# Attention and two feed-forward networks on one core: block 0 goes through both networks before the pair

## The chip, the core and the metric

The kernel runs on one core of a Trainium2 chip. The metric is the device time of one execution in microseconds. A core has TensorE (matmuls, PE below), VectorE (DVE), ScalarE (ACT), GpSimd (POOL) and SyncE (SP, whose one queue issues all transfers here). Every engine works through its own instructions in a fixed order and waits at semaphores for the others.

## The reference

Three stages in a row, all with float32 results:

```python
# 1 attention, 2 x 8 heads, 768 positions, 64 wide: a window of |i-j| < 16, and 24 block keys
k_sum = k.reshape(B, H, 24, 32, D).max(axis=3);  v_sum = v.reshape(B, H, 24, 32, D).mean(axis=3)
scores = concat(where(|i-j| < 16, q @ k.T / 8, -1e9), q @ k_sum.T / 8 + log(32))
x = softmax(scores) @ concat(v, v_sum)                       # 1536 tokens x 512
# 2 gated network, 512 -> 1536 -> 512
xn = x / sqrt(mean(x * x) + 1e-6) * rms_g
g = xn @ w_gate;  x = (g * sigmoid(g) * (xn @ w_val)) @ w_out
# 3 second network, 512 -> 2048 -> 512
h = x @ w_in;  out = where(h > 0, h, exp(min(h, 0)) - 1) @ w_out2
```

The five weight matrices arrive as 64-bit floats.

## The kernel before, in words

**Blocks.** The 1536 tokens are three blocks of 512. Block 0 goes through the first network alone (12 chunks of 128 hidden columns: g and v projections, gate, down product). Blocks 1 and 2 go through it as a *pair*: the up products are made by seven products of sums of parts instead of eight plain ones (Strassen's scheme in Winograd's form), where the parts are the two blocks and the two halves of the model dimension. For that each chunk needs sums of weight halves (`half_sum`, s1 to s4, four per chunk) and VectorE combines the seven product banks into four results (`add_combine`, seven additions and one copy). The second network is made in the same way: block 0 alone by seven products over its own halves with 256 columns each (`product`, L1084), the pair by seven with 512 columns (`pair_product`, L1237). There the sums of weights are whole tiles (`w_sum`, four per group of four chunks).

**Splitting.** Each factor of a matmul is split into a rounded high part and a remainder (`split_a` and `act_a` on ACT, L303; `split_b` and `act_b`, L314), and each product is three matmuls: high by high, high by low, low by high.

**Weights.** `fetch` loads 512 KB of 64-bit words into one of three staging buffers (`st`), four steps turn them into float32 (`convert_a` on ACT L432; `convert_b` L440 and `convert_d` L453 on VectorE), `keep` stores the tile in device memory, and `again` loads it back for a later use (`j0i`, `j0p` for block 0's second network, `j1...` for the pair). The first network's weights (g, v, o) are converted while block 0 goes through it; those of the second (i, p) from 40 us after the start of the pair's first network on, one every 5.6 us of the plan.

**Attention** is made in 12 pairs of 64-token tiles. The four pairs of block 0 and a part of the next come first, the others are strewn through block 0's first network, one pair every 14 us of the plan. From the eighth pair on (`HERE = 7`) the queries are loaded by 16 small transfers and transposed on VectorE (L527); before, they are loaded at once, transposed by TensorE (L501) and copied by ACT.

**What sets the order.** No order is written out. Every operation is added to a planner (`class Order`) with an engine (or a choice of engines), a cost, a due time and what it reads and writes; the planner plays the operations through with its own costs, takes on each free engine the ready one that is due first, and issues the instructions in the order that comes out. Due times follow from the starts of the chunks (`chunk1_at`, `joint1_at`, `chunk2_at`, `joint2_at`) and from a table of offsets, `SHIFT`, by operation and stage. The stages of the program are therefore: start and block 0's attention; block 0, first network; pair, first network; block 0, second network; pair, second network.

Of the kernel before, what the change touches and what calls it, by code (L numbers as in the profile page):

```python
# [10 lines left out]
F32 = mybir.dt.float32  # L11
F32R = mybir.dt.float32r
# [9 lines left out]
P = 128  # L22
# [195 lines left out]
def fused_kernel(ctx: ExitStack, tc: tile.TileContext, q, k, v, w_gate, w_val, w_out, rms_g, w_in2, w_out2, out):  # L218
    nc = tc.nc
# [17 lines left out]
    TB = 512  # L237
# [149 lines left out]
    joint1_at = [T0 + LEN_A * C1 + LEN_J * c for c in range(C1)]  # L387
    start2 = T0 + (LEN_A + LEN_J) * C1
    chunk2_at = [start2 + LEN_2 * c for c in range(C2)]
    joint2_at = [start2 + LEN_2 * C2 + LEN_U * u for u in range(U2)]  # L390
    tile_at = {}
    for i in range(B * NQ):
        blk, r = divmod(i, TPB)
        if blk == 0:
            tile_at[i] = A0 + A_GAP * r + (LATER if r >= TPB // 2 else 0) + TOFF[r]
        else:
            tile_at[i] = T0 + TILE8 + GAP_1 * (i - TPB)
# [6 lines left out]
    turn = [(kind, 4 * u + x) for u in range(U2) for kind in "ip" for x in range(4)]  # L404
    weights += [(kind, c, joint1_at[0] + CONV0 + CONV * n) for n, (kind, c) in enumerate(turn)]
# [49 lines left out]
    def add_weights(kind, c, need):  # L455
# [7 lines left out]
        add("SP", 0.75, need - 4, keep, kind, c, r=[raw], w=[f"kept_{kind}{c}"])  # L463
# [629 lines left out]

    def down2(b, u, m, n, first, last):
        ot = T[f"act2_{b}_{u}{m}{n}"]
        for j in range(2):
            wt = T[f"ws{b}_p{4 * u + 2 * m + j}"]
            for q in range(2):
                name = f"acc2_{b}_{2 * n + q}"
                acc = new(f"a{2 * n + q}", name, [P, TB]) if first and j == 0 else T[name]  # L1100
                cs = slice(j * HALF + q * P, j * HALF + (q + 1) * P)
                for x, (a, e) in enumerate(THREE):
                    nc.tensor.matmul(  # L1103
                        acc, ot[:, a, cs], wt[:, e, :],
                        start=first and j == x == 0, stop=last and j == 1 and x == 2)
# [20 lines left out]

    def add_block2():
        b = 0
        names = [f"acc2_{b}_{m}" for m in range(4)]
        src = [f"x1_{b}#n{c}_0" for c in range(KM)]  # L1130
        t0 = chunk2_at[0]

        def halves(name):
            return [f"xt{b}_{name}"] if name[0] == "t" else src[:2] if name[0] == "1" else src[2:]

        add("-", 0.0, t0 - 9, wait, w=[f"begin{b}"])
        for dst, at in (("t1", -3.2), ("t2", -2.6), ("t3", -1.0), ("t4", -0.5)):
            x, y = X_SUMS[dst]
            add(SUM_X, 0, t0 + at, x_sum, b, dst, r=halves(x) + halves(y) + [f"begin{b}"], w=[f"xt{b}_{dst}"], new=[(TMP, f"xt{b}_{dst}")])
        for i in range(7):  # L1140
            xq = f"xq{b}_{i}"
            at = t0 - 4 + 0.9 * i
            add({ACT: 0.52, DVE: 0.34}, 0, at, factor_a, b, i, r=halves(PAIRS[i]) + [f"begin{b}"], w=[xq + "#h"], new=[("x", xq)])
            add(SUM_X, 0, at + 0.5, factor_b, b, i, r=halves(PAIRS[i]) + [xq + "#h"], w=[xq + "#l"])
        for u in range(U2):
            t = chunk2_at[4 * u]
            n = f"{b}_{u}"
            for x in (2, 3, 0, 1):
                add_again(0, "i", 4 * u + x, t - 13 + 0.2 * x)
            add_sums(b, u, t)  # L1150
            tt = [t + STEP * i for i in range(7)]
            p = f"_{n}"
            for i in range(7):
                add_split(f"ws{n}_{i}", weight_of(b, u, i), tt[i], LO_1)
                bank = f"p{i}{p}"
                add(PE, 1.44, tt[i], product, b, u, i, bank, MM + AT,
                    r=[f"ws{n}_{i}#h", f"ws{n}_{i}#l", f"xq{b}_{i}#h", f"xq{b}_{i}#l"], w=[bank],
                    new=[(MM + AT, bank)])
            add_combine(p, tt, MM + AT)
            for k, (m, h, done) in enumerate(((0, 0, 1), (0, 1, 4), (1, 1, 5), (1, 0, 6))):  # L1160
                at = tt[done] + 2.3
                act = f"act2_{n}{m}{h}"
                add_elu(f"c{m}{h}{p}", f"ex{p}{m}{h}", act, at, "t2")
                if k in (0, 2):
                    for j in range(2):
                        x = 4 * u + 2 * m + j
                        add_again(0, "p", x, at + DOWN2[k] - 7)
                        add_split(f"ws{b}_p{x}", f"j0p{x}", at + DOWN2[k] + 0.7 * j, LO_1)
# [224 lines left out]
    for i in range(B * NQ):  # L1393
# [135 lines left out]
```

## Time and profile before

| | us |
|---|---|
| median of 3 runs | 656.55 |
| lowest, highest | 653.52, 662.18 |
| the profiled execution | 656.8 |
| its span in the trace | 655.1 |

| engine | busy us | share of the span |
|---|---|---|
| TensorE | 612.9 | 94% |
| VectorE | 562.1 | 86% |
| ScalarE | 379.2 | 58% |
| GpSimd | 210.2 | 32% |

The granted TensorE clock is 0.992 of full speed over the span. Neighbouring instructions of an engine overlap in the records (the end of one lies behind the start of the next), so the cost of one among others is read from start to start, not from its length. Busy time counts overlapped time once.

### The profile page before, as it was taken

The page shows a single profiled execution, that of the slowest core. Times are in us where ns is not written, and L with a number is a line of the kernel's source. Part 1 is how long each engine was busy: PE and PEld are TensorE (multiplying, and loading weights), DVE is VectorE, ACT ScalarE, POOL GpSimd, SP SyncE. Part 2 cuts the span into 40 slices and gives each one's busy share as a digit, 9 for nine tenths or more (in the row PEclk, how much of TensorE's full clock was granted, in tenths as well). Part 3 has the DMA queues.
Part 4 walks back from the last instruction along what each step waited for, and adds up shares of the span by engine and source line. Part 5 has one row for each costly group of instructions (what it writes and reads, how often), then busy time and mean ns, then how long its engine had stood idle before and what let it go on. Part 6 is the DMA issues. An engine that isn't in the chain of part 4 may idle for free.

```text
span 655.1 us, 10659 instructions
## 1 busy us (share of the span) xinstructions
PE 612.9 (94%) x3668; PEld 497.9 (76%) x3668; DVE 562.1 (86%) x961; ACT 379.2 (58%) x819; POOL 210.2 (32%) x240
## 2 busy tenths in 40 slices
PE   7689999779999999899889899999999999999997
PEld 4478866557778678677778687889887878888885
DVE  4788896569899999999999799989999996498665
ACT  2777866678838445455434545678675753355351
POOL 6763364444534324335225302331430210200000
PEclk9979999999999999999999899999999999999999
DMA  9999778779737238575546253534223211020003
GB/s 210 241 275 215 230 194 215 174 235 252 255 93 218 88 122 280 175 241 194 193 155 215 80 162 125 181 129 138 56 81 130 65 62 52 0 66 0 1 0 130
DMA packets 100454, 97.04 MB, mean 148 GB/s; under 512 B 54192, under 2 KB 69808, under 8 KB 100400
## 3 DMA queue, kind: packets, MB, share of 16 engines
q1 hardware_dynamic: 100400, 96.36, 51.1%
q8 instruction: 29, 0.48, 0.3%
q14 instruction: 25, 0.20, 0.1%
HBM read 75.37 MB, written 20.97 MB: 147 GB/s over the span
## 4 chain that ended last, share of the span: by engine, by line
PE 37%; DVE 29%; issue 3%; DMA 1%; ACT 1%; DVEq 0%
PE p_k L1237 10%; PE dn L1245 8%; PE acc L985 7%; PE acc L1103 5%; PE p L1084 4%; PE p_j L1237 3%; DVE c_j L1092 3%; DVE wj L314 3%; DVE h_j L1092 3%; DVE act_j L314 2%; DVE th_j L956 2%; DVE ws L314 2%; DVE th_j L952 2%; DVE raw_i L453 1%; DVE raw_p L453 1%
## 5 line engine op out<-in xcount | busy, mean ns | idle before, releaser
L1237 PE MATMUL p_j<-xh,wj 128*128 128x512 f32 x336 | 110.6, 395 | 8.3 <-DVE c_j L1092 3.8
L1237 PEld LDWEIGHTS p_j<-xh,wj 128*128 128x128 f32 x336 | 63.0, 188 | 27.3 <-DVE c_j L1092 5.6
L1237 PE MATMUL p_k<-xh,ws 128*128 128x512 f32 x224 | 71.7, 391 | 0.9 <-DVE h_k L1092 0.9
L1237 PE MATMUL p_j<-xl,wj 128*128 128x512 f32 x168 | 65.5, 390 | 0.0
L1237 PEld LDWEIGHTS p_k<-xh,ws 128*128 128x128 f32 x224 | 42.0, 188 | 10.7 <-DVE h_k L1092 1.0
L1277 POOL TENSOR_TENSOR sa<-j1v 128x256 f32<-128x256 f32 x12 | 18.4, 1530 | 92.4 <-DVE wj L314 45.0
L1103 PE MATMUL acc<-ws_p,act 128*128 128x512 f32 x192 | 45.8, 391 | 0.4 <-DVE act L314 0.4
L1245 PE MATMUL dn<-ws_p,act_k 128*128 128x512 f32 x192 | 45.8, 389 | 0.0
L985 PE MATMUL acc<-ws_p,act_k 128*128 128x512 f32 x192 | 45.5, 389 | 0.0
L1084 PEld LDWEIGHTS p<-xq,ws 128*128 128x128 f32 x336 | 42.3, 191 | 2.7 <-issue 1.6
L1084 PE MATMUL p<-xq,ws 128*128 128x256 f32 x336 | 42.9, 283 | 1.4 <-DVE x L1251 1.4
L1237 PE MATMUL p_k<-xl,ws 128*128 128x512 f32 x112 | 43.7, 390 | 0.3 <-DVE xl L1206 0.3
L1245 PEld LDWEIGHTS dn<-ws_p,act_k 128*128 128x128 f32 x192 | 36.0, 188 | 7.6
L985 PEld LDWEIGHTS acc<-ws_p,act_k 128*128 128x128 f32 x192 | 36.0, 188 | 7.5
L1103 PEld LDWEIGHTS acc<-ws_p,act 128*128 128x128 f32 x192 | 35.5, 188 | 7.9 <-DVE act L314 0.9
L948 ACT ACTIVATE th_j<-c_j 128x512 f32<-128x512 f32 x24 | 15.2, 633 | 43.5 <-DVE c_j L1092 43.4
L1245 PE MATMUL dn<-act_j,wjo 128*128 128x512 f32 x144 | 36.5, 406 | 3.0 <-DVE h_j L1092 1.9
L919 PE MATMUL pg<-xs,ws_g 128*128 128x512 f32 (+1 forms) x168 | 37.8, 369 | 0.8 <-POOL ws_g L314 0.8
L1044 POOL TENSOR_TENSOR w_s<-j1i,j1i 128x512 f32<-128x512 f32 x8 | 13.0, 1624 | 78.1 <-DVE ws_p L314 48.6
L985 PE MATMUL acc<-act_j,wjo 128*128 128x512 f32 x144 | 36.2, 391 | 1.2 <-DVE act_j L314 1.2
L985 PE MATMUL acc<-act,ws_o 128*128 128x512 f32 x144 | 36.2, 397 | 0.4 <-DVE act L314 0.2
L1251 DVE TENSOR_TENSOR ob<-ob,dn 128x512 f32<-128x512 f32 x28 | 19.0, 684 | 20.2 <-PE dn L1245 20.2
(292 smaller groups left out, 1568.8 us busy)
## 6 DMA issues: line engine op xcount, KB each, us to landing
st_i<-in_moe_w_in SPq DMA_DIRECT2D x16, 512.0 KB, 4.1
st_p<-in_moe_w_out SPq DMA_DIRECT2D x16, 512.0 KB, 3.8
st_g<-in_moe_w_gate SPq DMA_DIRECT2D x12, 512.0 KB, 4.6
st_v<-in_moe_w_val SPq DMA_DIRECT2D x12, 512.0 KB, 5.9
st_o<-in_moe_w_out SPq DMA_DIRECT2D x12, 512.0 KB, 4.3
kept_i<-raw_i SPq DMA_DIRECT2D x16, 256.0 KB, 2.2
kept_p<-raw_p SPq DMA_DIRECT2D x16, 256.0 KB, 2.3
j0i<-kept_i SPq DMA_DIRECT2D x16, 256.0 KB, 3.1
```

The lines of the kernel that those rows point to most:

```text
L314: (nc.gpsimd if eng == POOL else nc.vector).tensor_sub(out, a, b)
L453: nc.vector.scalar_tensor_tensor(low, rest, 2.0 ** -13, low, op0=ALU.mult, op1=ALU.add)
L919: nc.tensor.matmul(pt[:, i], wt[:, a, kk * P:(kk + 1) * P], xt[:, c, i], start=(kk == 0 and n == 0), stop=(kk == KM - 1 and n == 2))
L948: nc.scalar.activation(out=new(tag, th, [P, TB]), in_=T[pg], func=AF.Tanh, scale=0.5)
L985: nc.tensor.matmul(acc, lhsT, rhs, start=(first and n == 0), stop=(last and n == 2))
L1084: nc.tensor.matmul(pt[:, m * HALF:(m + 1) * HALF], wt[:, a, kk * HALF + m * P:kk * HALF + (m + 1) * P], xt[:, c, kk], start=kk == n == 0, ...
L1092: nc.vector.tensor_add(new(TMP, dst, [P, TB]), T[src], T[other])
L1103: nc.tensor.matmul(acc, ot[:, a, cs], wt[:, e, :], start=first and j == x == 0, stop=last and j == 1 and x == 2)
L1237: nc.tensor.matmul(pt, wt[:, a, cs], xt[e][:, kk], start=kk == n == 0, stop=kk == 1 and n == 2)
L1245: nc.tensor.matmul(pt, lhsT, rhs, start=x == n == 0, stop=x == len(pairs) - 1 and n == 2)
L1251: nc.vector.tensor_add(T[dst][:, m], T[dst][:, m], T[src])
L1277: (e.tensor_add if dst == "s1" else e.tensor_sub)(t[:, i * HALF:(i + 1) * HALF], x, y)
```

## The change

1. **Order of the stages.** Block 0 goes through the first and then the second network, and only then does the pair start: block 0, first; block 0, second; pair, first; pair, second. The second network's weights are fetched and converted in block 0's second network and used there at once, without `again`. Tiles of block 1 lie in block 0's first network, those of block 2 in its second.
2. **Block 0's second up product is plain** (`project2`): per chunk 12 matmuls of 512 columns, no sums, no combining.
3. **Sums of weights on VectorE**: `half_sum` and `w_sum` go from GpSimd to VectorE.
4. **Queries turned by TensorE**: `HERE` from 7 to 12, so all twelve are.
5. **Plan refitted**: `SHIFT`, its stage limits `EDGES`, and some lengths are new; `keep` is issued 3 us behind a weight's need instead of 4 ahead.

```diff
-    SUM_W = {POOL: 1.28}
+    SUM_W = {DVE: 0.6}
-    SUM_H = {POOL: 0.8}
+    SUM_H = {DVE: 0.335}
...
-    joint1_at = [T0 + LEN_A * C1 + LEN_J * c for c in range(C1)]
-    start2 = T0 + (LEN_A + LEN_J) * C1
+    start2 = T0 + LEN_A * C1
     chunk2_at = [start2 + LEN_2 * c for c in range(C2)]
-    joint2_at = [start2 + LEN_2 * C2 + LEN_U * u for u in range(U2)]
+    pair1 = start2 + LEN_2 * C2
+    joint1_at = [pair1 + LEN_J * c for c in range(C1)]
+    joint2_at = [pair1 + LEN_J * C1 + LEN_U * u for u in range(U2)]
...
-    turn = [(kind, 4 * u + x) for u in range(U2) for kind in "ip" for x in range(4)]
-    weights += [(kind, c, joint1_at[0] + CONV0 + CONV * n) for n, (kind, c) in enumerate(turn)]
+    for c in range(C2):
+        weights += [("i", c, chunk2_at[c // 2 * 2] - 2 + 0.8 * (c % 2)), ("p", c, chunk2_at[c] + 4)]
...
-        add("SP", 0.75, need - 4, keep, kind, c, r=[raw], w=[f"kept_{kind}{c}"])
+        add("SP", 0.75, need + KEEP, keep, kind, c, r=[raw], w=[f"kept_{kind}{c}"])
...
+    def project2(name, u, h, m):
+        pt = new(MM, name, [P, TB])
+        for k in range(2):
+            wt = T[f"ws0_i{4 * u + 2 * h + k}"]
+            for kk in range(2):
+                cs = slice(kk * HALF + m * P, kk * HALF + (m + 1) * P)
+                xt = T[f"xa_{2 * k + kk}"]
+                for n, (a, e) in enumerate(THREE):
+                    nc.tensor.matmul(pt, wt[:, a, cs], xt[:, e], start=k == kk == n == 0, stop=k == kk == 1 and n == 2)
...
+        add_x("x1_0", "xa", 0, TB, chunk2_at[0] - 3)
+        x = [f"xa_{kk}#{p}0" for kk in range(KM) for p in "hl"]
+        for c in range(C2):
...
+            add(PE, 2.72, t, project2, ph, u, h, m, r=x + [y + z for y in w for z in ("#h", "#l")], w=[ph], new=[(MM, ph)])
+            add_elu(ph, ex, act, t + 2.8, "t2")
+            add_split(wp, f"raw_p{c}", t + 6, LO_1)
+            add_down(names, act, wp, c == 0, c == C2 - 1, False, t + DOWN2)
...
     add_block1()
+    add_block2()
     add_joint1()
-    add_block2()
     add_joint2()
...
-    ('copy_k', 0): -3, ('copy_keys', 0): -8, ('copy_q', 0): -2, ('diagonal', 0): -8, ('exps', 0): 0.5,
+    ('copy_k', 0): 18.5, ('copy_keys', 0): -11, ('diagonal', 0): 25, ('exps', 0): 28, ('load_q', 0): 3.5,
...
-HERE, KHERE, TURNED, ACT_B = 7, 6, 0.48, 0
+HERE, KHERE, TURNED, ACT_B = 12, 6, 0.48, 0
-LEN_A, LEN_J, LEN_2, LEN_U = 10.5, 15.0, 5.3, 41.0
+LEN_A, LEN_J, LEN_2, LEN_U = 9.3, 15.0, 6.3, 41.0
```

Three places in the instruction order. First VectorE in the middle of the pair's first network (`p_j` are the product banks, `h_j` and `c_j` the partial and finished combinations, `th_j` the gate, `wj` split weights, `sa` and `sb` the half sums, `raw_i` weights under conversion). Before:

```order
L952 SCALAR_TENSOR_TENSOR th_j_3967<-th_j_3967,c_j_3964 128x512
L453 SCALAR_TENSOR_TENSOR raw_i_3933<-st_i_3832,raw_i_3933 128x512
L956 SCALAR_TENSOR_TENSOR th_j_3967<-th_j_3967,c_j_3977 128x512
L314 TENSOR_TENSOR wj_1_3979<-sa_3935,wj_1_3979 128x512
L314 TENSOR_TENSOR wj_2_3990<-sb_3962,wj_2_3990 128x512
L314 TENSOR_TENSOR act_j_4008<-th_j_3967,act_j_4008 128x512
L440 TENSOR_SCALAR raw_i_4026<-st_i_3894 128x512
L314 TENSOR_TENSOR wj_3_4023<-j1v_3761,wj_3_4023 128x256
```

and now:

```order
L1203 TENSOR_TENSOR sb_4148<-j1g_3997,sa_4102 128x256
L1203 TENSOR_TENSOR sa_4151<-j1v_3896 128x256
L1203 TENSOR_TENSOR sb_4148<-j1g_3997,j1v_3988 128x256
L1203 TENSOR_TENSOR sa_4151<-sa_4151,j1g_3907 128x256
L1052 TENSOR_TENSOR h_j_4161<-p_j_4109,h_j_4135 128x512
L1203 TENSOR_TENSOR sb_4165<-j1g_3907,sa_4151 128x256
L314 TENSOR_TENSOR wj_1_4163<-sa_4151,wj_1_4163 128x512
L1203 TENSOR_TENSOR sb_4165<-j1g_3907,j1v_3896 128x256
L1052 TENSOR_TENSOR c_j_4183<-p_j_4168,h_j_4161 128x512
```

The conversions are gone from this stretch, and half sums stand in their place, always ahead of the split that reads them.

Second, TensorE where block 0 leaves the first network (`acc` are the down sums). Before, the pair's products (`p_j`) follow, which read nothing of block 0:

```order
L985 MATMUL acc_0_0_1500<-act_0_8_2527,ws_o_2357 128x512 x3
L985 MATMUL acc_0_1_1504<-act_0_8_2527,ws_o_2357 128x512 x3
L860 MATMUL prs2slice(0, 512, None)_2759<-dg2slice(0, 512, None)h,ones 128x512
L860 MATMUL prs2slice(0, 512, None)_2759<-dg2slice(0, 512, None)l,ones 128x512
L1237 MATMUL p_j_2762<-xh_0_2448,wj_0_2744 128x512
```

and now block 0's own second network (`ph`), whose input `xa` is split from the finished sums:

```order
L974 MATMUL acc_0_0_1230<-act_0_11_2504,ws_o_2314 128x512 x3
L974 MATMUL acc_0_1_1234<-act_0_11_2504,ws_o_2314 128x512 x3
L974 MATMUL acc_0_2_1435<-act_0_11_2504,ws_o_2314 128x512 x3
L974 MATMUL acc_0_3_1439<-act_0_11_2504,ws_o_2314 128x512 x3
L736 MATMUL at_3_0_2566<-ident,e_3_0_2357 120x128 x4
L736 MATMUL at_3_1_2575<-ident,e_3_1_2358 120x128 x4
L502 MATMUL qt_5_2587<-ident,qr_5_2467 128x128 x4
L748 MATMUL pv_3_2597<-ats_3_0_2582,va_179 64x64
...
L1082 MATMUL ph_2623<-xa_2564,ws_i_2377 128x512 x3
```

Between the last sum and the first product that needs it stand three groups of transposes and one tile product.

Third, TensorE where the pair leaves the first network (`dn_11` are the last down sums of block 2, gathered on VectorE). Before, block 0's products (`p_0_0`, `p_0_1`) lie between them:

```order
L1084 MATMUL p_0_0_4869<-xq_5_4533,ws_0_5_4747 128x256 x12
L1084 MATMUL p_0_0_4888<-xq_6_4536,ws_0_6_4777 128x256 x12
L1245 MATMUL dn_11_2_4917<-act_j_4336,wjo_4221 128x512 x3
L1245 MATMUL dn_11_2_4917<-act_j_4511,wjo_4348 128x512 x3
L1245 MATMUL dn_11_2_4917<-act_j_4685,wjo_4635 128x512 x3
L1084 MATMUL p_0_1_4937<-xq_0_4479,ws_1_0_4819 128x256 x12
```

and now the pair's second network (`p_k`), which reads the sums:

```order
L974 MATMUL acc_1_3_3903<-act_j_5265,wjo_5164 128x512 x3
L1171 MATMUL dn_11_1_5305<-act_j_5009,wjo_4915 128x512 x3
L1171 MATMUL dn_11_1_5305<-act_j_5190,wjo_5046 128x512 x3
L1171 MATMUL dn_11_1_5305<-act_j_5262,wjo_5164 128x512 x3
L1171 MATMUL dn_11_2_5324<-act_j_5009,wjo_4915 128x512 x3
L1171 MATMUL dn_11_2_5324<-act_j_5190,wjo_5046 128x512 x3
L1171 MATMUL dn_11_2_5324<-act_j_5262,wjo_5164 128x512 x3
L1163 MATMUL p_k_5340<-xh_0_5303,ws_0_0_5135 128x512
```

18 matmuls of 512 columns stand between block 1's last sum (`acc_1_3`) and the first product of the next network.

## Rows read from the trace of the kernel before

**Rows 1.** Stages: us, busy us (instructions) by engine, clock, DMA share, GB/s

```profile
0.00:49.88 49.88, 38.98 (x506) 28.76 (x507) 34.04 (x80) 30.41 (x102) 33.22 (x86) 0.93 1.08 243
49.88:190.09 140.21, 128.62 (x1083) 102.40 (x1082) 111.53 (x228) 101.78 (x278) 67.29 (x78) 1.00 0.78 210
190.09:387.60 197.51, 186.11 (x805) 148.51 (x804) 192.87 (x311) 98.47 (x179) 65.57 (x48) 0.99 0.54 176
387.60:479.79 92.19, 89.30 (x536) 79.18 (x535) 89.08 (x139) 63.05 (x113) 25.53 (x16) 1.00 0.42 129
479.79:655.10 175.31, 169.89 (x745) 139.09 (x743) 134.58 (x208) 85.50 (x150) 18.57 (x12) 1.00 0.16 50
sum 655.10, PE 612.89 PEld 497.95 DVE 562.09 ACT 379.22 POOL 210.19; mean PE 122.58 PEld 99.59 DVE 112.42 ACT 75.84 POOL 42.04
```

**Rows 2.** Waits: who waited, for whom, us in total, times, longest

```profile
PE p_j L1237 <- DVE c_j L1092: 3.8, 4, 1.9
...
PE s L695 <- DVE qT L527: 3.1, 1, 3.1
...
DVE qT L527 <- DMA qr<-in_q: 11.1, 3, 5.0
```

**Rows 3.** Timeline, DVE and POOL around 315 us: start, length, instruction

```profile
313.15 1.23 DVE L314 TENSOR_TENSOR act_j<-th_j,act_j 128x512 fp32r<-128x512 f32 x1
314.31 0.95 DVE L440 TENSOR_SCALAR raw_i<-st_i 128x512 uint32<-128x512 uint32 x1
315.19 0.95 DVE L314 TENSOR_TENSOR wj<-j1v,wj 128x256 fp32r<-128x256 f32 x1
316.06 1.26 DVE L453 SCALAR_TENSOR_TENSOR raw_i<-st_i,raw_i 128x512 uint16<-128x512 uint16 x1
317.22 0.67 DVE L1251 TENSOR_TENSOR x<-x,dn 128x512 f32<-128x512 f32 x1
...
312.77 1.06 POOL L1277 TENSOR_TENSOR sa<-j1v 128x256 f32<-128x256 f32 x1 [6.48 <-DVE wj L314]
...
315.82 0.91 POOL L1277 TENSOR_TENSOR sb<-j1g,j1v 128x256 f32<-128x256 f32 x1
```

**Rows 4.** Timeline, DVE and POOL around 301 us

```profile
299.76 0.42 DVE L314 TENSOR_TENSOR wj<-j1v,wj 128x256 fp32r<-128x256 f32 x1
300.10 0.69 DVE L956 SCALAR_TENSOR_TENSOR th_j<-th_j,c_j 128x512 f32<-128x512 f32 x1
300.70 0.42 DVE L440 TENSOR_SCALAR raw_p<-st_p 128x512 uint32<-128x512 uint32 x1
301.04 0.69 DVE L1092 TENSOR_TENSOR c_j<-p_j,h_j 128x512 f32<-128x512 f32 x1
301.64 0.75 DVE L453 SCALAR_TENSOR_TENSOR raw_p<-st_p,raw_p 128x512 uint16<-128x512 uint16 x1
302.27 0.68 DVE L956 SCALAR_TENSOR_TENSOR th_j<-th_j,c_j 128x512 f32<-128x512 f32 x1
...
301.68 4.61 POOL L1277 TENSOR_TENSOR sb<-j1g,j1v 128x256 f32<-128x256 f32 x1
```

**Rows 5.** Timeline of PE at two places, and the query transposes' group (busy us, mean ns)

```profile
547.18 11.04 PE L985 MATMUL acc<-ws_p,act_k 128*128 128x512 f32 x48
558.06 2.88 PE L1245 MATMUL dn<-ws_p,act_k 128*128 128x512 f32 x12
...
389.17 1.60 PE L1084 MATMUL p<-xq,ws 128*128 128x256 f32 x12
390.61 2.23 PE L1245 MATMUL dn<-act_j,wjo 128*128 128x512 f32 x9
...
L501 PE MATMUL qt<-ident,qr 128*128 128x128 f32 x28 | 4.3, 283 | 0.0
```

**Rows 6.** The 16-bit addition of the conversions in the pair's first network (DVE busy us)

```profile
190.09:387.60 197.51, 22.77 (x26) 0.99 0.54 176
```

**Rows 7.** DMA queue of the transfers: packets, MB, share of 16 engines

```profile
q1 hardware_dynamic: 100400, 96.36, 51.1%
```

More of the change, by code (lines that the diff above doesn't have):

```diff
@@ L1092, in combine @@
         nc.vector.tensor_add(new(TMP, dst, [P, TB]), T[src], T[other])
[L1094 to L1105, printed above, removed]
     def add_combine(p, tt, tags):
@@ L1125, in add_elu @@
         add_act(ex, act, at + 1.8)
-    def add_block2():
[L1128 to L1168, printed above, removed]
-                first, last = u == 0 and k < 2, u == U2 - 1 and k >= 2
-                add(PE, 2.72, at + DOWN2[k], down2, b, u, m, h, first, last,
-                    r=[act + "#h", act + "#l"] + [f"ws{b}_p{4 * u + 2 * m + j}#{x}" for j in range(2) for x in "hl"],
-                    w=[f"acc2_{b}_{2 * h + q}" for q in range(2)],
-                    new=[(f"a{2 * h + q}", f"acc2_{b}_{2 * h + q}") for q in range(2)] if first else [])
-        add_out(b, names, chunk2_at[-1] + 8, (2, 3, 0, 1))
@@ L1484 @@
-    ('fetch', 8): -1, ('gate_a', 8): 3, ('gate_b2', 8): 1.5, ('gate_c2', 8): -17, ('gather', 8): 50,
-    ('keep', 8): 7, ('pair_a', 8): 0.5, ('pair_b', 8): 32, ('pair_product', 8): -1, ('pair_sum', 8): -3,
-    ('product', 8): -7.5, ('save', 8): -1, ('split_a', 8): 6, ('split_b', 8): -1, ('w_sum', 8): 3,
-    ('wait', 8): -4, ('x_sum', 8): -7.5, ('act_b', 9): -8, ('again', 9): -17, ('combine', 9): -22.5,
-    ('copy_out', 9): -6.5, ('down', 9): -3.5, ('down2', 9): 2, ('down_part', 9): 3, ('elu_a', 9): -7,
@@ new lines @@
+    ('down', 3): 23, ('exps', 3): 81, ('fetch', 3): 2, ('gate_a', 3): 10.5, ('gate_b', 3): 13,
+    ('gate_c', 3): 1.5, ('guard', 3): -15.5, ('invert', 3): -10.5, ('keep', 3): -10.5, ('load_k', 3): -50.5,
+    ('load_q', 3): 21, ('load_v', 3): -27, ('load_vtok', 3): -120, ('max_k', 3): 9.5, ('mean_v', 3): 20.5,
+    ('normalize', 3): 12.5, ('project', 3): 9.5, ('row_max', 3): -7.5, ('scores', 3): -2, ('split_a', 3): -15,
+    ('split_b', 3): 3, ('take', 3): -21, ('turn_e', 3): -5, ('turn_k', 3): -217, ('turn_q', 3): 8.5,
@@ new lines @@
+    ('sum_square', 5): 2, ('take', 5): -18.5, ('turn_e', 5): -6.5, ('turn_q', 5): 16, ('x_hi', 5): -1.5,
+    ('x_lo', 5): 12, ('act_a', 6): 10, ('act_b', 6): -37.5, ('add_mask', 6): 6, ('apply_v2', 6): 35,
+    ('convert_a', 6): -17, ('convert_b', 6): 4.5, ('convert_d', 6): 6.5, ('copy_e', 6): -61,
+    ('copy_keys', 6): -0.5, ('copy_q', 6): -5, ('copy_x2', 6): 1.5, ('down', 6): 183.5, ('elu_a', 6): -3.5,
+    ('elu_c', 6): 8, ('exps', 6): 3, ('fetch', 6): -6.5, ('guard', 6): 2, ('keep', 6): 47, ('load_q', 6): 0.5,
@@ new lines @@
+    ('sum_square', 7): -2, ('turn_e', 7): 3.5, ('turn_q', 7): -5, ('wait', 7): -3.5, ('zero_v', 7): 6,
+    ('act_a', 8): -4, ('act_b', 8): 19.5, ('combine', 8): 31.5, ('copy_out', 8): -1.5, ('down', 8): -16,
+    ('down_part', 8): 5, ('gate_a', 8): -17, ('gate_b2', 8): -1, ('gather', 8): -9, ('half_sum', 8): 21.5,
+    ('keep', 8): -0.5, ('pair_b', 8): 6, ('pair_sum', 8): -57, ('save', 8): 14, ('split_a', 8): -3,
+    ('split_b', 8): -3, ('store', 8): -27, ('take', 8): 6, ('act_a', 9): 6, ('act_b', 9): -4.5,
@@ new lines @@
+    ('pair_b', 10): -4.5, ('pair_product', 10): -5, ('pair_sum', 10): 20.5, ('save', 10): -0.5,
+    ('split_a', 10): -2, ('split_b', 10): -5, ('w_sum', 10): 2, ('wait', 10): -10.5, ('act_a', 11): 24.5,
+    ('act_b', 11): 12.5, ('again', 11): 2.5, ('combine', 11): 1, ('copy_out', 11): -21,
+    ('down_part', 11): 29.5, ('elu_a', 11): -4.5, ('elu_c', 11): -16.5, ('gather', 11): 28.5,
+    ('pair_product', 11): -166, ('split_a', 11): 1.5, ('store', 11): 7.5, ('store_part', 11): 10.5,
+    ('take', 11): -5.5, ('w_sum', 11): 7,
```

159 lines of the change are left out of this document (62 added, 97 removed).

## The prediction

> **What bounds the kernel now.** I read the busy time by stage first, then the waits of TensorE, then the order of time of VectorE and GpSimd at one spot. The stages are cut at TensorE's first product of each: start, block 0 through the first network (with the tiles of blocks 1 and 2), the pair's first network, block 0's second network, the pair's second network [rows 1]. The reader should see that TensorE is busy 612.9 us in all and idle 42.2: 10.9, 11.6, 11.4, 2.9 and 5.4 us by stage. So whatever the change does, only those gaps and the work itself can move. VectorE is busy 192.9 of 197.5 us in the pair's first network and 89.1 of 92.2 in the stage behind it: there it is as full as TensorE, while in the last stage it has 40 us to spare.
>
> The waits say what the gaps are [rows 2]: in the pair's first network TensorE waits for combined products and gathers on VectorE, in block 0's first network for tiles, the largest being 3.1 us for queries that VectorE transposes; VectorE itself stood 11.1 us there for the small query loads.
>
> Then the spot [rows 3]. Four VectorE instructions from 313.15 to 317.22 us took 4.07 us while GpSimd ran four half sums. At the pace at which such instructions start when GpSimd doesn't hold them up [rows 4] they need 0.60 + 0.34 + 0.34 + 0.63 = 1.91 us (0.60 for 512 columns, 0.34 for 256 or for the shift, 0.63 for the 16-bit add). So VectorE lost 2.16 us, 0.54 us for each half sum that GpSimd does "beside" it.
>
> **TensorE's work.** Its pace: 48 matmuls of 512 columns in 10.88 us, 0.2267 us each; 12 of 256 columns in 1.44 us [rows 5].
> - Block 0's up product: out go 28 groups of 12 narrow matmuls, 28 x 1.44 = 40.3 us; in come 16 x 12 wide ones, 192 x 0.2267 = 43.5 us. Plus 3.2 us.
> - Queries: five more groups of four transposes at 4.3/7 = 0.61 us [rows 5], plus 3.1 us. Out goes the 3.1 us wait for them [rows 2].
>
> So TensorE's work grows by some 6 us, and a gain must come from gaps. I split the program at the pair's first product (190.09 us before), since the order shows what stands on either side.
>
> **Up to the pair's first product.** By the order, 748 wide matmuls stand ahead of it instead of 346; the narrow ones there are the same. Added: 402 x 0.2267 = 91.1 us. Transposes +3.1, query wait -3.1. The other 8.5 us of gaps of block 0's first network belong to tiles; the same eight pairs of tiles now lie in twice the time, and I take half off, -4.2 (bounds: 0, -8.5). The queue of the first 50 us is reordered (second-batch keys come ahead of the second weights); nothing in the trace prices that, so 0, with bounds of -4 and +4, about a third of that stage's 10.9 us of gaps. New: block 0's second network starts when all four sums of the first are copied and split: four copies on two engines (1.2 us on each), then on VectorE two splits priced like a shift at 0.34 and four remainders at 0.60, 4.3 us with its copies; beside it lie three groups of four transposes at 0.61, one tile product and the last 1.4 us of the sums, over 3.2 us. That leaves about 1; with the hand-overs +1.5 (0 to 3).
>
> VectorE must also keep up there. A chunk of the second network costs TensorE 24 x 0.2267 = 5.4 us, and VectorE two conversions (0.97 each), two splits, one ELU and one remainder, 4.3 us; 16 of them 69 us, beside tile work. That is about 85% with the tiles, in order, and GpSimd still works for the tiles: +3 (0 to 10). The conversions of the second network's weights move here from the pair's first network. The first product of the pair then stands at 190.1 + 91.1 - 4.2 + 1.5 + 3 = 281.5 us.
>
> **From there to the end.** By the order 1,536 wide matmuls: 348.2 us. Before, 1,746 wide and 336 narrow ones (395.8 + 40.3 = 436.1 us) took 465.0: 28.9 us lost. Of these the last stage lost 175.3 - 744 x 0.2267 = 6.6, its store included; the 22.3 others lie where VectorE was 97% busy. A chunk of the pair's first network now costs VectorE 18 instructions at 0.60 and five at 0.34 (the four half sums among them), 12.5 us, against 66 x 0.2267 = 15.0 us on TensorE: 84% instead of 98%. The 26 conversions that lay in it (0.97 us each, 25 us) [rows 6] are gone. I therefore price it near the last stage, where VectorE is 77% busy: 5 us lost (3 to 15).
>
> The second network's weight sums also move to VectorE: 16 x 0.60 = 9.6 us on top of 134.6 in 175.3 [rows 1]. Covered by its 40 us of idle time, so 0; if the cover goes, 9.6.
>
> Block 0's products used to fill TensorE while the pair's last sums were gathered. Now the pair's second network follows at once. The order puts 18 wide matmuls (4.1 us) between the last sum and the first product, and nine more two products later; VectorE has some fifteen instructions of 0.60 in that stretch, all of which must be in time: +2 (0 to 5).
>
> Sum: 281.5 + 348.2 + 5 + 2 + 6.6 = 643.3, and 1.7 us lie outside the span (656.8 against 655.1): **645 us**. The profiled execution is 0.25 us above the median of the runs shown, so no correction.
>
> **DMA.** 32 re-loads of block 0's weights go (32 x 128 x 512 numbers of 4 bytes = 8.4 MB of 96.4) [rows 7]; the many small query loads become five large ones. But 32 fetches and their stores move ahead of the pair. I count 96.4 - 8.4 = 88.0 MB in all, less the re-loads and outputs behind the pair's first product (some 18.5) and 12.1 in the start (49.9 us at 243 GB/s): 57 MB in 232 us, 246 GB/s. Block 0's first network ran at 210 GB/s with the DMA engines 78% busy [rows 1], which leaves room to 270. Taken as hidden; see the third rival. The store of each converted weight is issued some 7 us later in the plan; its buffer is held that long.
>
> **Rivals.**
> 1. *VectorE stays the bound of the pair* (0.17). The Trainium skill, Perfetto Trace Analysis, section Optimizing Scalar/DVE Operations, says that where VectorE is saturated, handing work to ScalarE or even GpSimd may make sense, which speaks against taking the half sums back; the same passage adds that between GpSimd and VectorE it might not help, as they share a port. As a mechanism of this kernel: if GpSimd's sums cost VectorE nothing, its 192.9 us in the pair's first network become 192.9 - 25 (its conversions) + 48 x 0.34 = 184 us, more than TensorE's 12 x 15.0 = 179.5, and the gaps of 11.4 us stay instead of 5: with the seam, 653 us. Against it: the 0.54 us of [rows 3]; for it: that is one spot, and from 299.8 to 302.3 us VectorE keeps its pace while GpSimd is the one held up, 4.61 us for one half sum [rows 4].
> 2. *All gaps close* (0.15). The other half of the tile waits goes too (-4.2), the pair loses 2 us and the seams nothing (-3, -3.5): 634 us. For it: the last stage runs so already.
> 3. *The loads bound block 0* (0.08, the slower end). All weights are now read before the pair, through one in-order queue and three staging buffers. If that stretch moves no more than the 210 GB/s of block 0's first network, 57 MB need 271 us instead of 232, and the time is 684; at 225 GB/s 666. It decides from about 240 GB/s down. Against it: that stage held eight pairs of tiles and the small query loads, and the pair's stage moved 176 GB/s at 54% [rows 1].
> 4. *The fit doesn't carry over*: seams and the second network at their upper bounds (+1.5, +7, +3): 656, inside "no change" (0.05).
>
> **How the numbers follow.** The forecast of 645 has 0.55, with its own range of 638 to 653 from the terms above. About 2% (13 us, so 643.4 and 669.7) is what a measurement of this kernel can tell from no change; the forecast is just short of it. Faster by over 2%: rival 2 and somewhat under half of the forecast, 0.15 + 0.25 = 0.40. Slower: rival 3 below 222 GB/s, 0.07. Within: 0.53. The range reaches from 633 to 659, leaving out a part of rival 2 and rival 3.
>
> **What would show it.** Right: the pair's first product near 281 us; VectorE 80 to 88% busy behind it with no instruction above 0.8 us there; TensorE idle under 8 us between that product and the pair's second network; one gap of 1 to 3 us where block 0's second network starts. Wrong: the first product later than 292 us with DMA share above 0.9 (rival 3) or VectorE above 95% (the +3 too small); TensorE waiting for combined products as before (rival 1); a gap over 5 us at the pair's seam; a start that is not within 4 us of 50.

## The result and the profile after

The changed kernel takes **629.7 us** (median of 4 runs, 627.9 to 632.7) against 655.2 of the kernel before (four runs by now): ratio 0.960, 95% interval 0.952 to 0.968. The forecast was 645 with a range of 633 to 659: too slow by 15 us, and the time lies below the range. The profiled execution took 630.45 us with a span of 628.7.

By stage, cut at the first product of each (start; block 0, first; block 0, second; pair, first; pair, second), with the columns of [rows 1]:

```profile
0.00:51.24 51.24, 40.58 (x510) 29.34 (x511) 32.74 (x79) 29.36 (x97) 30.73 (x84) 0.90 1.09 235
51.24:182.31 131.07, 128.55 (x983) 104.77 (x982) 116.31 (x219) 99.65 (x252) 55.87 (x63) 1.00 0.88 265
182.31:274.40 92.09, 90.94 (x522) 74.28 (x519) 88.09 (x165) 76.10 (x162) 11.30 (x12) 1.00 0.75 247
274.40:457.56 183.16, 183.16 (x808) 151.29 (x807) 165.82 (x295) 77.17 (x135) 0.00 (x0) 1.00 0.21 64
457.56:628.70 171.14, 166.36 (x730) 136.06 (x728) 137.94 (x223) 89.08 (x157) 0.00 (x0) 1.00 0.15 44
sum 628.70, PE 609.59 PEld 495.73 DVE 540.89 ACT 371.38 POOL 97.90; mean PE 121.92 PEld 99.15 DVE 108.18 ACT 74.28 POOL 19.58
```

TensorE is idle 19.1 us instead of 42.2. In the order of the lines it is idle 10.7, 2.5, 1.2, 0.0 and 4.8 us; in the same stages before it was 10.9, 11.6, 2.9, 11.4 and 5.4. So about half of the gain lies in the pair's first network and most of the rest in block 0's first. The fourth line is the pair's: 183.16 us with TensorE busy for all of it. Its 807 matmuls (the 808th in the line is the next stage's first) need 807 x 0.2267 = 182.9 us; almost nothing is lost. VectorE is busy 165.8 us there, 91% of the stage.

The waits turned round. In [rows 2] TensorE waited for VectorE's combined products; now the longest waits of VectorE in that stage are for TensorE, and what TensorE waits for in block 0's first network is small (columns as in [rows 2]):

```profile
DVE c_j L1052 <- PE p_j L1163: 10.1, 16, 2.2
...
PE qt L502 <- ACT ats L303: 1.0, 1, 1.0
PE pg L920 <- DVE th L941: 0.7, 1, 0.7
```

VectorE in the stretch that answers to [rows 3]: the half sums stand among the other instructions, the next one starts about 0.60 us behind one of 512 columns and 0.33 us behind one of 256, and none is longer than 0.69:

```profile
308.43 0.42 DVE L1203 TENSOR_TENSOR sa<-j1v 128x256 f32<-128x256 f32 x1
308.76 0.69 DVE L1052 TENSOR_TENSOR h_j<-p_j,h_j 128x512 f32<-128x512 f32 x1
309.36 0.42 DVE L1203 TENSOR_TENSOR sa<-sa,j1g 128x256 f32<-128x256 f32 x1
309.69 0.69 DVE L1052 TENSOR_TENSOR c_j<-p_j,h_j 128x512 f32<-128x512 f32 x1
310.30 0.42 DVE L1203 TENSOR_TENSOR sb<-j1g,sa 128x256 f32<-128x256 f32 x1
310.63 0.69 DVE L314 TENSOR_TENSOR wj<-sa,wj 128x512 fp32r<-128x512 f32 x1
```

The two seams on TensorE. Where block 0 leaves the first network it waits 1.03 us, for a copy of a tile; `ph` itself then starts without a gap. Where the pair leaves it, there is no gap:

```profile
178.57 1.03 PE L736 MATMUL at<-ident,e 128*120 128x128 f32 x8
180.63 0.66 PE L502 MATMUL qt<-ident,qr 128*128 128x128 f32 x4 [1.03 <-ACT ats L303]
181.22 1.15 PE L748 MATMUL pv<-ats,va 120*64 120x64 f32 x32
182.31 1.89 PE L1082 MATMUL ph<-xa,ws_i 128*128 128x512 f32 x7
...
450.76 2.88 PE L974 MATMUL acc<-act_j,wjo 128*128 128x512 f32 x12
453.48 4.24 PE L1171 MATMUL dn<-act_j,wjo 128*128 128x512 f32 x18
457.56 0.39 PE L1163 MATMUL p_k<-xh,ws 128*128 128x512 f32 x1
```

The transfers did not bind: block 0's stages moved 265 and 247 GB/s, where the third rival needed 246. The queue carried less than in [rows 7], as counted:

```profile
q1 hardware_dynamic: 89472, 87.97, 48.1%
```

### The profile page after: what moved, and what is told of

Its sections match the earlier page's. It is cut to its first block, busy times and chain, and to the rows that moved or that the text cites. A ratio compares the mean times of both kernels' runs of the same rounds, so it can differ in the third digit from the quotient of the medians.

```text
span 628.7 us, 10064 instructions
## 1 busy us (share of the span) xinstructions
PE 609.6 (97%) x3544; PEld 495.7 (79%) x3544; DVE 540.9 (86%) x976; ACT 371.4 (59%) x800; POOL 97.9 (16%) x159
## 3 DMA queue, kind: packets, MB, share of 16 engines
q1 hardware_dynamic: 89472, 87.97, 48.1%
## 4 chain that ended last, share of the span: by engine, by line
PE 78%; DVE 9%; DMA 4%; ACT 3%; SPq 3%; issue 2%; ACTq 0%; DVEq 0%
PE acc L974 21%; PE p_j L1163 18%; PE p_k L1163 12%; PE dn L1171 12%; PE ph L1082 6%; PE pg L920 2%; DMA va<-in_v 2%; ACT e L713 1%; PE pv L748 1%; DMA st_i<-in_moe_w_in 1%; PE at L736 1%; PE s L696 1%; DVE xT L867 1%; SPq L506 1%; SPq L652 1%
## 5 line engine op out<-in xcount | busy, mean ns | idle before, releaser
L1163 PE MATMUL p_j<-xh,wj 128*128 128x512 f32 x336 | 107.5, 389 | 0.0
L1082 PE MATMUL ph<-xa,ws_i 128*128 128x512 f32 x192 | 45.9, 393 | 1.1 <-DVE ex L954 1.1
L1082 PEld LDWEIGHTS ph<-xa,ws_i 128*128 128x128 f32 x192 | 35.6, 188 | 9.2 <-DVE ex L954 1.6
L1052 DVE TENSOR_TENSOR c_j<-p_j,h_j 128x512 f32<-128x512 f32 x48 | 32.8, 687 | 10.2 <-PE p_j L1163 10.1
L1163 PEld LDWEIGHTS p_j<-xl,wj 128*128 128x128 f32 x168 | 31.5, 188 | 6.4
L1171 PE MATMUL dn<-act_j,wjo 128*128 128x512 f32 x144 | 35.1, 391 | 0.0
L920 PEld LDWEIGHTS pg<-xs,ws_g 128*128 128x128 f32 x168 | 27.6, 189 | 5.9 <-DVE th L941 1.1
L1171 PEld LDWEIGHTS dn<-act_j,wjo 128*128 128x128 f32 x144 | 26.9, 188 | 6.0 <-DVE c_j L1052 0.3
```

Source lines behind the costliest of these rows:

```text
L920: nc.tensor.matmul(pt[:, i], wt[:, a, kk * P:(kk + 1) * P], xt[:, c, i], start=(kk == 0 and n == 0), stop=(kk == KM - 1 and n == 2))
L1052: nc.vector.tensor_add(new(TMP, dst, [P, TB]), T[src], T[other])
L1082: nc.tensor.matmul(pt, wt[:, a, cs], xt[:, e], start=k == kk == n == 0, stop=k == kk == 1 and n == 2)
L1163: nc.tensor.matmul(pt, wt[:, a, cs], xt[e][:, kk], start=kk == n == 0, stop=kk == 1 and n == 2)
L1171: nc.tensor.matmul(pt, lhsT, rhs, start=x == n == 0, stop=x == len(pairs) - 1 and n == 2)
```

## The experiments

Theory 1: VectorE's work in the pair's first network made the gaps there; the change takes it out (25 us of conversions; GpSimd's half sums with the time they take from VectorE). Theory 2: the refitted table of offsets made the gain. Medians; the ratio is to the kernel before on the same chip.

| run | us | ratio, 95% interval |
|---|---|---|
| b_dve_all | 651.5 | 0.995 [0.992, 0.998] |
| b_nolow | 642.5 | 0.981 [0.976, 0.986] |
| b_nolow_dve | 636.5 | 0.972 [0.967, 0.977] |
| b_plain | 652.5 | 0.998 [0.994, 1.001] |
| b_dve_half | 654.5 | 1.001 [0.998, 1.003] |
| b_here12 | 649.4 | 0.989 [0.983, 0.994] |
| b_noshift | 672.8 | 1.026 [1.021, 1.031] |
| after | 629.7 | 0.960 [0.952, 0.968] |
| a_pool_half | 632.7 | 0.964 [0.960, 0.968] |
| a_dve12 | 633.9 | 0.968 [0.963, 0.974] |
| a_dve25 | 647.1 | 0.985 [0.981, 0.989] |
| a_pool_dve25 | 652.0 | 0.994 [0.991, 0.997] |
| a_gp48 | 643.6 | 0.985 [0.982, 0.988] |
| a_noshift | 650.1 | 0.990 [0.987, 0.994] |
| a_tiles1 | 648.0 | 0.990 [0.985, 0.995] |

### Taking VectorE's work out of the kernel before

b_nolow leaves the 16-bit additions of the second network's weights out:

```diff
     def convert_d(kind, c):
+        if kind in "ip":
+            return
```

b_dve_all does this in `half_sum` and `w_sum`, b_dve_half in `half_sum` alone:

```diff
-        e = nc.gpsimd if eng == POOL else nc.vector
+        e = nc.vector
```

b_nolow: 

> The kernel before, with the 16-bit addition of the second network's 32 weight tiles left out (the low words of those weights are left out of the computation); order and everything else as they were. It takes 26 x 0.60 = 15.6 us of VectorE's time out of the pair's first network. Theory 1: the stage falls from 197.5 us to 189 to 192, the total by 5 to 9 us. Theory 2: VectorE's time isn't what TensorE waited for, and the stage stays within 2 us of 197.5.

b_dve_all: 

> The kernel before, with its plan and its order as they were, but all sums of weights (half sums and whole ones) issued on VectorE instead of GpSimd at the place where they stood. Theory 1 (VectorE's time made the gaps, and a half sum on GpSimd takes 0.54 us of it where VectorE needs 0.34 itself): in the pair's first network VectorE falls from 192.9 us to about 192.9 - 48 x 0.54 + 48 x 0.34 = 183 us, its instructions' mean lengths fall to about 0.69 us, and the stage shortens from 197.5 us to 189 to 193; the total falls by 4 to 9 us. Theory 2 (the new order and its refitted plan made the gain, VectorE's load didn't): the stage stays at 197 us or grows, since VectorE now has 48 instructions more in an order that wasn't made for them; the total is 0 to 8 us higher.

b_nolow_dve (both edits): 

> Both at once on the kernel before: the 16-bit addition of the second network's weights left out, and all sums of weights on VectorE. Theory 1: VectorE at about 168 us in the pair's first network, whose 11.4 us of idle TensorE shrink to 1 to 3 us; stage 187 to 189 us, total 9 to 12 us below the kernel before, which is the share of the 25 us that the pair's first network gave. Theory 2: within 3 us of the kernel before.

Measured, each from the pair's first product to its second network (the pair's first network and block 0's second together, with the same matmuls; columns of [rows 1]): before, all sums moved, additions left out, both:

```profile
190.09:479.79 289.70, 275.41 (x1339) 227.69 (x1338) 281.95 (x449) 161.52 (x292) 91.10 (x64) 0.99 0.50 161
```
```profile
192.00:477.21 285.21, 275.96 (x1339) 226.02 (x1338) 283.97 (x510) 161.72 (x291) 0.00 (x0) 1.00 0.49 164
```
```profile
187.77:464.94 277.17, 271.94 (x1339) 227.04 (x1338) 265.05 (x417) 161.09 (x292) 71.26 (x64) 1.00 0.51 168
```
```profile
188.20:460.84 272.64, 270.35 (x1339) 227.62 (x1338) 265.80 (x478) 160.55 (x291) 0.00 (x0) 1.00 0.52 171
```

The stretch shrinks by 4.5, 12.5 and 17.1 us. So without any new order or plan, most of the 22.3 us that the prediction counted as lost there comes back once the additions and the sums are gone. The additions alone gave more than expected (12.5 against 5 to 9): theory 1 in direction, its size too small. But look at VectorE's busy time: moving the sums did not lower it, 282.0 to 284.0 and 265.1 to 265.8. The relief that follows from the prediction's price for them (48 x (0.54 - 0.34) = 9.6 us) isn't there. The last two lines also have the same VectorE time and lengths 4.5 us apart, so the sum of VectorE's work alone does not set the loss. Which sums gave the 4.5 us was asked next.

b_dve_half: 

> The kernel before with only the half sums on VectorE; the whole-tile sums of the second network stay on GpSimd. With both moved the stretch from the pair's first product to its second network went from 289.7 to 285.2 us and the total from 655.1 to 651.5. If the half sums made that gain: 285 to 287 us for the stretch, total 650 to 653. If the whole-tile sums (16 on GpSimd in block 0's second network, 12 behind it) made it: 289 to 290 us, total 654 to 657.

It gave no change in the total (1.001), though the stretch of its one profile is 2.9 us shorter: what b_dve_all gave, 3.6 us in the median, is not shown to come from the half sums. Whether it is the whole-tile ones (a_pool_dve25 below points that way), and by what wait, stays open.

### Putting work back into the changed kernel

Here `more` is the reloaded weight tile that the half sum reads, and `spare` a tile that nothing reads.

```diff
# a_pool_half (in half_sum; a_pool_dve25 also in w_sum)
+        e = nc.gpsimd
# a_dve25, a_pool_dve25; in a_dve12 only for s1 and s3
+        nc.vector.tensor_add(spare[:, :440], more[:, :440], more[:, :440])
# a_gp48
+        nc.gpsimd.tensor_add(spare[:, :256], more[:, :256], more[:, 256:])
```

a_pool_half: 

> The changed kernel with the half sums issued on GpSimd again (the whole-tile sums stay on VectorE), in the same order and at the same places. Theory 1: VectorE's 165.9 us in the pair's first network become 165.9 - 48 x 0.34 + 48 x 0.54 = 175.5 us, its mean lengths of instructions rise to 0.8 us, but 175.5 is still below TensorE's 183.2, so the stage grows by only 1 to 4 us. If GpSimd holds VectorE up for the whole of each half sum (1.33 us each by the kernel before's 65.6 us in 48), VectorE needs 166 - 16 + 64 = 214 us and the stage grows by about 31 us. If GpSimd's sums cost VectorE nothing (rival 1's ground), VectorE falls to 150 us and the stage stays at 183 to 184 us. Theory 2: no change either.

a_dve25: 

> The changed kernel with 25 us more of VectorE's work in the pair's first network: behind each of the 48 half sums one more addition of 440 columns (about 0.525 us) into a tile that nothing reads, as long in sum as the conversions that the change took out of the stage. Theory 1: VectorE needs 166 + 25 = 191 us, more than TensorE's 183.2, and becomes the bound: the stage is 191 to 196 us, TensorE idle for 8 to 12 us of it. Theory 2 (the fitted order hides such work): the stage grows by less than 3 us.

a_pool_dve25: 

> The changed kernel with both loads of the kernel before put back on the pair's first network: all sums of weights on GpSimd, and 25 us more of VectorE's work (48 additions of 440 columns into a tile that nothing reads). Theory 1: VectorE needs 175.5 + 25 = 200 us; the stage is 200 to 206 us, 17 to 22 us longer, and the order of the stages and its fit have gained nothing there that this load doesn't take back. Theory 2: the stage grows by under 6 us.

a_dve12: 

> The changed kernel with half of the earlier extra load: one more addition of 440 columns (0.53 us) on VectorE behind every second half sum, 24 in all, 12.7 us, into a tile that nothing reads. VectorE then needs 165.9 + 12.7 = 178.6 us of the pair's first network against TensorE's 183.2. If VectorE costs time only where its sum of work exceeds TensorE's (theory 1 in its plain form), the stage stays within 1 us of 183.2. If the two engines hold each other up well before that (theory 1 with a knee: 25 us of extra load cost 16.2 us, not the 8 that its sum exceeds TensorE's by), the stage is 187 to 192 us.

a_gp48: 

> The changed kernel, all its own sums left on VectorE, with 48 more half sums (256 columns) on GpSimd into a tile that nothing reads, one beside each half sum of the pair's first network. VectorE's own instructions are the same as in the changed kernel, so what they lengthen by is what GpSimd takes from VectorE. If that is 0.54 us for each (the step on record), VectorE has 26 us more, as with the 25 us of extra additions (+16.2 us in the stage): stage 196 to 201 us, VectorE busy some 190. If it is about 0.28 us (summed from the mean lengths in the kernel before), 13 us more, as with the 12.7 us of extra additions (+6.1): stage 187 to 191 us. If nothing: 183 to 184 us. Instructions that read or write product banks keep 0.685 us in every case, as they did in the earlier runs; those between tiles alone lengthen.

The pair's first network (after: 183.16) in a_pool_half, a_dve12, a_dve25, a_pool_dve25 and a_gp48, in this order:

```profile
276.45:463.29 186.84, 185.00 (x809) 150.86 (x809) 160.99 (x253) 77.86 (x138) 46.46 (x42) 1.00 0.21 64
```
```profile
278.01:467.27 189.26, 186.27 (x809) 150.19 (x807) 176.98 (x319) 77.66 (x137) 0.00 (x0) 1.00 0.21 63
```
```profile
273.38:472.74 199.36, 189.09 (x808) 149.71 (x808) 188.31 (x341) 77.55 (x138) 0.00 (x0) 1.00 0.20 60
```
```profile
274.70:473.62 198.92, 189.69 (x808) 149.37 (x808) 189.03 (x293) 77.90 (x138) 55.67 (x49) 1.00 0.19 60
```
```profile
276.84:472.26 195.42, 189.32 (x808) 152.28 (x808) 178.91 (x297) 78.40 (x138) 35.28 (x36) 0.99 0.20 61
```

- The dose: 0, 12.7 and 25 us more of VectorE's work, of which VectorE's busy time shows 11.2 and 22.5 us in this stage, make it 183.2, 189.3 and 199.4 us. The plain form of theory 1 (loss only above 183.2 us of work) fails: at 188.3 us of VectorE's time 16 are lost, not 5, and at 177.0 us already 6. The 6 rest on one trace, that of the longest of four runs, 5 us above their median; by the medians the total grew by 4.2 us, and the intervals overlap with after's. What shows the cause is who TensorE waits for there (a_dve12, then a_dve25; columns of [rows 2]; after has no such wait):

```profile
PE p_j L1164 <- DVE h_j L1053: 1.6, 2, 1.4
```
```profile
PE p_j L1164 <- DVE h_j L1053: 3.7, 4, 2.4
PE p_j L1164 <- DVE x L1178: 2.8, 3, 1.4
```

- The 25 us cost 17 us in the total, two thirds of what the change gave.
- a_pool_dve25 was expected at 200 to 206 us in this stage and took 198.9, no more than a_dve25: with VectorE full, four half sums per chunk cost as much on GpSimd as on VectorE. Its extra 5 us in the total lie in the last stage (176.6 us against a_dve25's 170.0), where the whole-tile sums are on GpSimd again.
- a_pool_half: 3.7 us longer in the profile, within the 1 to 4 expected, but not for the reason given: VectorE's busy time fell to 161.0 us where 175.5 was expected. After's 165.8 us less its 44 half sums of this stage (18.0 us) leave 147.8; the 42 on GpSimd cost VectorE the other 13.2, about 0.31 us each. What makes the 3.7 us stays open; by the medians the intervals overlap with after's.
- a_gp48 prices a GpSimd half sum. VectorE does the same work as in after, and its busy time grows by 13.1 us here and by 3.9 in the stage ahead (88.1 to 92.0), where the first 12 lie: 17.0 / 48 = 0.35 us each, between the two expectations, and no less than the 0.34 that VectorE needs to do the sum itself. The two stages grow by 16.4 us. The 13.1 us cost this stage 12.3 us (195.4), more than the 187 to 191 expected for so much.

Which instructions pay shows in a_gp48's timeline of VectorE and GpSimd (start, length, instruction):

```profile
299.92 0.96 DVE L1204 TENSOR_TENSOR sa<-j1v 128x256 f32<-128x256 f32 x1
300.81 2.35 DVE L315 TENSOR_TENSOR act_j<-th_j,act_j 128x512 fp32r<-128x512 f32 x2
303.09 0.95 DVE L1204 TENSOR_TENSOR sa<-sa,j1g 128x256 f32<-128x256 f32 x1
303.96 0.68 DVE L1053 TENSOR_TENSOR c_j<-p_j,h_j 128x512 f32<-128x512 f32 x1
304.56 0.68 DVE L1053 TENSOR_TENSOR h_j<-p_j,h_j 128x512 f32<-128x512 f32 x1
305.16 0.85 DVE L315 TENSOR_TENSOR wj<-sa,wj 128x512 fp32r<-128x512 f32 x1
...
299.66 1.83 POOL L1206 TENSOR_TENSOR spare<-j1g 128x256 f32<-128x256 f32 x2 [3.55 <-DMA j1g<-kept_g]
301.56 2.19 POOL L1206 TENSOR_TENSOR spare<-j1v 128x256 f32<-128x256 f32 x2
303.83 1.63 POOL L1206 TENSOR_TENSOR spare<-j1g 128x256 f32<-128x256 f32 x2
```

While GpSimd works, a sum of 256 columns between tiles takes 0.96 us instead of 0.42 and `act_j` 1.18 instead of 0.69; the two that read a product bank (`p_j`) right beside it keep 0.68. The 0.54 us of [rows 3] was taken from four instructions between tiles, the kind that pays.

### The order, the tiles and the queries

a_noshift and b_noshift empty the table (`SHIFT = {}`), b_here12 sets `HERE = 12` in the kernel before, a_tiles1 sets `tile_at[i] = T0 + TILE8 + 7.0 * (i - TPB)` for blocks 1 and 2, and b_plain puts `project2` with its twelve wide matmuls into the kernel before.

a_noshift: 

> The changed kernel with its whole table of offsets emptied, so that the planner orders by the bare due times. The kernel before without its own table isn't timed here, so this is read by stages. Theory 1: the pair's first network has 17 us of VectorE to spare and keeps below 3 us of idle TensorE without any fit; losses come where tiles lie (start and block 0, +5 to +15 us) and at the seams. Theory 2: the pair's first network loses as much as it did before, 8 us or more.

b_noshift: 

> The kernel before with its whole table of offsets emptied, to stand beside the changed kernel with an empty table (650.1 us). Theory 1 (what the stages hold makes the gain): without any fit the kernel before loses about what the changed one lost by it, and stands some 25 us above 650: 668 to 682 us. Theory 2 (the refitted table makes the gain): both structures are equal without a table: 645 to 657 us.

Without a table the structures are 22.7 us apart (672.8 and 650.1), with their tables 25: theory 2 falls for the total; the tables are worth about as much to either (17 and 20 us). The other planning constants stayed as each kernel has them. In the profiles much of that growth is TensorE's busy time, at a lower granted clock: b_noshift is busy 623.7 us at 0.969 (before: 612.9 at 0.992), a_noshift 618.3 at 0.984. But theory 1's expectation for the stage failed too, and theory 2's (8 us or more) came true there. The pair's first network in a_noshift:

```profile
282.12:474.25 192.13, 186.36 (x808) 152.14 (x807) 173.19 (x307) 82.94 (x147) 0.00 (x0) 0.99 0.21 65
```

It loses 192.1 - 182.9 = 9.2 us, 4.1 of it waiting for split weights, with VectorE busy 90%. Room on VectorE is needed and not enough; the order must use it.

b_here12: 

> The kernel before with one part of the change alone: all queries turned by TensorE (five more groups of transposes, 3.1 us), none by VectorE; the table of offsets as it was. If the waits for tiles in block 0's first network come from the query loads and VectorE's transposes, that stage (140.2 us, 11.6 idle) loses its 3.1 us wait and some of the other 8.5, gains 3.1 us of transposes and is 133 to 139 us long. If they come from too many tiles in one network, it stays at 139 to 143 us.

Block 0's first network:

```profile
49.52:183.83 134.31, 126.26 (x1081) 102.84 (x1080) 105.33 (x214) 102.80 (x275) 66.50 (x78) 0.97 0.82 226
```

It fell from 140.2 to 134.3 us, TensorE idle 8.1 instead of 11.6. Not all of the 5.9 us is gained: with 20 transposes more the stage has two matmuls fewer, since 22 of them (12 wide down products, 2.7 us, among them) now come behind the pair's first product. The total fell by 6.2 us (ratio 0.983 to 0.994). So the query turn was worth more than its 3.1 us wait, which the prediction had set against the transposes at nothing.

a_tiles1: 

> The changed kernel with the due times of the tiles as they were before: all eight pairs of tiles of blocks 1 and 2 are due every 14 us through block 0's first network, instead of four there and four in its second; everything else, the table of offsets too, as in the changed kernel. Now the first network has 2.5 us of idle TensorE and the second 1.2 us. If spreading the tiles over both networks closed the gaps, the two stages together (223.2 us) grow by 5 to 9 us, in waits for tiles. If the query turns or the better fit closed them, they stay within 3 us of 223 (some may come from the table not being fitted to this).

Block 0's first and second network:

```profile
55.87:207.09 151.22, 143.05 (x1138) 115.34 (x1136) 126.08 (x251) 114.46 (x299) 65.16 (x80) 0.97 0.79 236
207.09:296.35 89.26, 88.30 (x386) 71.69 (x384) 84.56 (x152) 65.41 (x120) 0.00 (x0) 1.00 0.73 246
```

The two stages took 240.5 us instead of 223.2, more than expected. Of the 17.3 us, 5.5 are idle time (8.2 in the first network, as much as in b_here12); the rest is busy time, with 19 matmuls more (4.3 us if all are wide) and a granted clock of 0.97 in the first network. The total is 18 us up, 4.6 of it in the start, where a key load is waited for 5.2 us. The table wasn't fitted to this, so the direction is shown and the size isn't.

b_plain: 

> The kernel before with one part of the change alone: block 0's second up product is plain (12 matmuls of 512 columns per chunk, no sums, no combining), order of the stages, conversions and GpSimd's half sums as before; due times as they were. It takes about 34 us of VectorE's work and 16 GpSimd sums out of block 0's second network and adds 3.2 us of matmuls. If VectorE made the 2.9 us of gaps of that stage (theory 1), they shrink to about 1 us, and the total moves by +3.2 - 2 = about +1 us: -2 to +4. If the plan matters (theory 2), the unfitted order costs more than that: +4 to +12 us.

Block 0's second network:

```profile
379.80:463.08 83.28, 83.28 (x368) 68.46 (x366) 53.49 (x86) 48.83 (x89) 5.38 (x4) 1.00 0.35 111
```

It has no idle TensorE at all, with VectorE busy 53.5 us. The stage is shorter also because the last one has 42 matmuls more (787 against 745); the total fell by only 2.5 us, which its interval doesn't tell from none.

No version here beats the changed kernel.

## Why the prediction was wrong

The mechanism was right for the pair (VectorE's gaps go when the conversions leave its first network); it was the sizes of what remains that failed. Rival 2 ("all gaps close", 634 us, given 0.15) came nearest and is still 4 us too slow: it kept the 3 us for VectorE in block 0's second network, and TensorE's busy time as forecast.

1. **Up to the pair's first product**: forecast 281.5, measured 274.4. The start came 1.4 later. Of the 8.5 us that lie behind it, 5.1 are idle time: the terms -4.2, +1.5 and +3 left 8.8 us of it in block 0's two networks, and 3.7 are there. The step that failed first is "I take half off": 2.5 us of idle time are left in the first network, 1.0 of them at the seam. Turning the queries alone took 3.5 us of idle time out of that stage and 6.2 off the total, where the prediction had it at nothing, and with all tiles in one network 8.2 us of idle time come back. The seam's +1.5 was 1.0, for another cause; of the +3 for VectorE 1.1 came (one wait of `ph`), with VectorE busy 88.1 of 92.1 us. The other 3.3 us are TensorE's own: 222.8 busy us forecast, 219.5 measured, for the same number of matmuls (1,505); why these took less isn't shown.
2. **"5 us lost" in the pair**: measured 0.2. This step failed by its choice of row. The last stage's 6.6 us were read as what TensorE loses beside a VectorE at 77%. After the change that stage loses 171.14 - 728 x 0.2267 = 6.1 us still, and the stage ahead, with VectorE at 91%, nothing. The last matmuls end at 615.63 + 8.32 = 623.95 us of 628.7, so 4.8 of the 6.1 lie behind them, at the program's end, and say nothing of VectorE:

```profile
615.63 8.32 PE L1171 MATMUL dn<-ws_p,act_k 128*128 128x512 f32 x36
```

3. **The pair's seam, +2**: measured 0.
4. **The half sums** (0.54 us back for 0.34): one spot, of the kind of instruction that pays most. Measured 0.35 in a_gp48 and about 0.31 in a_pool_half, for 0.34: neutral. The Trainium skill, Perfetto Trace Analysis, section Optimizing Scalar/DVE Operations, named with the first rival, adds that moving work between GpSimd and VectorE might not help; the runs agree for the half sums (b_dve_half 1.001, a_pool_half's interval overlaps with after's).
5. **VectorE's load** in the pair's first network: 84% forecast, 165.8 / 183.2 = 91% measured. The chunk's 23 instructions are as counted; 27 others of the stage (splits and copies at its two ends), some 16 us, were left out. Too low, yet the loss was overpriced.
6. Right: matmul counts, the plain product's small weight, transfers hidden (87.97 MB against 88.0 forecast), whole-tile sums covered by VectorE's idle time in the last stage (137.9 of 171.1 us).

Points 1 to 3 and the end make up the 14.6 us between 643.3 and 628.7: 7.1 ahead of the pair's first product, 7.5 behind it. The single edits on the kernel before (additions 12.6, queries 6.2, sums 3.6, plain product 2.5) add up to 25 us, the size of the gain, but in part by luck: b_nolow leaves out work that the change only moves, the 2.5 isn't told from none, and that they add is shown only for the additions and the sums (16.2 apart, 18.6 together).

## What to carry to other kernels

Before pricing the gaps that remain, ask of the row that the price is taken from whether it has the same cause: a stage's loss at its end says nothing of its middle. Two engines that feed each other in fixed orders can lose time before either is full (a_dve12, with 97% as much work on VectorE as on TensorE, one trace). Where there is room (91%) a fitted order lost nothing and an unfitted one 9 us. So price the order as well as the load, and give "all gaps close" a fair chance when the relief is large (here 27 of VectorE's 193 us). Test one spot's stretched instructions against the group's mean before multiplying.

## What the runs showed that was not expected

- GpSimd lengthened only those VectorE instructions that take all operands from tiles. In a_gp48 `c_j` and `h_j`, which read product banks, keep 0.685 and 0.681 us in the mean over the stage, while `act_j` rises from 0.686 to 0.772 and `wjo` to 0.867. The Trainium skill, SBUF — State Buffer, section SBUF: two separate sides, says that a VectorE instruction with two inputs in SBUF and a GpSimd instruction that reads SBUF exclude each other for a whole instruction. The traces agree on which instructions pay; VectorE paid 13.1 us here for 35.3 us of GpSimd's work.
- 17 us of VectorE's time taken in that way cost the two stages 16.4 us (a_gp48); plain additions that kept VectorE busy 11.2 and 22.5 us longer cost 6.1 and 16.2 (a_dve12, a_dve25), so some 11 would be estimated for 17 from these. Where the time is taken seems to matter as well as how much; with one trace of each this isn't more than a sign, and why these spots are dearer stays open.
